# Window attention and two feed-forward layers on one core: both groups' products together in a visit, and three engines tied to the program's order

## The chip, the cores and the metric

The kernel runs on one core of one Trainium2 chip. The metric is the device time of one execution in microseconds (us). The core's engines are TensorE (PE: matmuls and transposes, with its weight loads as PEld), VectorE (DVE), ScalarE (ACT), GpSimd (POOL) and SyncE (SP, which here issues every DMA). Each takes its instructions from a queue of its own, and semaphores make one engine wait for another.

## The reference

Three layers follow each other. Attention with 4 batches, 8 heads, 576 positions and 64 channels, in which each position sees itself and the 63 before it; then x (2304 x 512) goes through a layer with three input matrices and an elementwise maximum, and through a second layer with a quadratic gate.

```python
scores = scale * np.matmul(q, k.transpose(0, 1, 3, 2))
mask = (rel >= 0) & (rel < window)                 # window = 64
attn = softmax(np.where(mask, scores, -1e9))
x = np.matmul(attn, v)                             # as 2304 tokens x 512
h = np.maximum(np.maximum(x @ w1, x @ w2), x @ w3) # 2304 x 768
x2 = h @ w_out                                     # 2304 x 512
h2 = x2 @ w_in                                     # 2304 x 2048
g = np.where(h2 >= 1, h2, np.where(h2 <= -1, 0, (h2 + 1) ** 2 / 4))
out = g @ w_out2
```

## The kernel before

Matmuls are in float32; each operand of a dense layer is split into a rounded high part and a rest, and three of the four products are taken. The first layer works on nine blocks of 256 tokens. For a block, 18 `a_item`s (line 357; 12 matmuls each, into one of three PSUM tiles `ps` of the pool `pmm`) make three products per slice f of the hidden layer. The first is copied out by ACT (`ht`), the other two are taken into a maximum by DVE (line 372), and a sixth of h is then split by ACT and POOL. Four `b_item`s (line 380; 18 matmuls) make x2, which ACT copies to one of two buffers `x2s` and SP stores to memory. The second layer (lines 536 to 633) works on blocks of 512 tokens; its weights are split by ACT, DVE and POOL (`w_split`, line 154), as those of the first layer are in the first 90 us.

Attention works on 36 groups of 64 positions (all heads). A group passes through load, `prep` (transposes of q and k, by PE for the first 16 groups, by DVE from `raw` tiles for the others), `qk` (line 275: 16 small matmuls for four pairs of heads into `sps2`; then DVE reads each pair, adds the mask and keeps the row's extreme in `nm`), `ex` (ACT, four exponentials), `norm` (DVE, then POOL multiplies), `ptr` and `ptc` (PE transposes, ACT copies to `pt`), and `pv` (line 334: 16 small matmuls into `ops2`; ACT copies the high part to the block's `xt`, DVE writes the rest). `sps2` takes two PSUM banks: a group's four pairs are spread over both, and the two groups of a visit stand in the same banks. `ops2` is one bank for both groups.

Groups 8 to 35 go through in 14 pairs. A list `order` holds pieces of work with a position each (an `a_item` takes 1, a `b_item` 1.5), and pairs are put at `visits` (line 505), 6 apart at first and then 12. At one visit stand PV of one pair, the transposes of the next, and QK of the one after. The list is sorted, and from the first visit on `chained` (line 549) keeps PE's instructions in the list's order (`issue_after`: order in the queue only, no wait). The other engines' orders are left to a scheduler that simulates the time. The tile framework lets two engines use one PSUM bank only after each other: it adds a semaphore wait wherever one follows the other in the list.

Of the kernel before, what the change touches and what calls it, by code (L numbers as in the profile page):

```python
# [9 lines left out]
F32 = mybir.dt.float32  # L10
# [24 lines left out]
BD = 6  # L35
# [10 lines left out]
VISITS = (-24, -18, -12)  # L46
VSTEP = 12
VLEAD = 2
EXP = (1.1, 2.1)
PTC = (0.6, 1.6)  # L50


# [8 lines left out]
def kernel(ctx, tc, q, k, v, w1, w2, w3, wo1, wi2, wo2, out, x2d):  # L61
# [12 lines left out]
    nc = tc.nc  # L74
# [7 lines left out]
    P = 128  # L82
    BL = 64
    NBB = S // BL
    NG = B * NBB
    NP = H // 2
# [20 lines left out]
    def act_copy(dst, src, scale=1.0):  # L107
        nc.scalar.activation(dst, src, AF.Copy, scale=scale)  # L108

    def sub(eng, dst, a, b):  # L110
        eng.tensor_tensor(dst, a, b, op=ALU.subtract)  # L111

    def f32(ap):
        return ap.bitcast(F32)
# [12 lines left out]
    apool = att_stack.enter_context(tc.tile_pool(name="apool", bufs=1, side="right", reuse_waits="tile"))  # L127
# [8 lines left out]
    ops2 = patt.tile([P, 2, NP, BL], F32, name="ops2")  # L136
# [37 lines left out]
    def w_col(key, hl, kt):  # L174
        return wslot[key][:, hl * 512 + kt * P: hl * 512 + (kt + 1) * P]


    st_g = defaultdict(dict)
# [4 lines left out]
    def blk(g):  # L183
        b, i = divmod(g, NBB)
        return b, i, g % 4

    def natural(g):
        return g % 4 != 0
# [77 lines left out]
    def window(g):  # L266

        b, i, s = blk(g)
        if i == 0:
            return lambda r, p: kring[r, p, s, :], maskA[:, BL:2 * BL], BL  # L270
        if natural(g):
            return lambda r, p: kring[r, p, s - 1:s + 1, :], maskA, 2 * BL
        return lambda r, p: kring[r, p, 0::3, :], maskB, 2 * BL

    def qk(g):
        d = st_g[g]
        win, mask, W = window(g)
        sm = apool.tile([P, NP, 2 * BL], F32, tag="sm", name="sm", bufs=5)
        nm = apool.tile([P, NP], F32, tag="nm", name="nm", bufs=5)


        for x in range(2):
            for bank in range(2):
                p = 2 * bank + x
                for h in range(2):
                    r = slice(h * BL, h * BL + BL)
                    o = (h ^ bank) * BL
                    nc.tensor.matmul(  # L288
                        sps2[o:o + BL, bank, g % 2, x, 0:W], d["q"][r, p, :], win(r, p), start=True, stop=True
                    )  # L290

        for p in range(NP):
            nc.vector.tensor_tensor_reduce(  # L293
                out=sm[:, p, 0:W], in0=sps2[:, p // 2, g % 2, p % 2, 0:W], in1=mask, scale=-QSCALE, scalar=BIG,
                op0=ALU.add, op1=ALU.min, accum_out=nm[:, p:p + 1],
            )
        d.update(sm=sm, nm=nm, W=W)

    def ex(g):
        d = st_g[g]  # L300
        W, sm = d["W"], d["sm"]
        ss = apool.tile([P, NP], F32, tag="ss", name="ss", bufs=5)
        for p in range(NP):
            nc.scalar.activation(  # L304
                sm[:, p, 0:W], sm[:, p, 0:W], AF.Exp, bias=d["nm"][:, p:p + 1], scale=-1.0, accum_out=ss[:, p:p + 1]
            )
        d["ss"] = ss

    def norm(g):
        d = st_g[g]  # L310
# [20 lines left out]
        act_copy(pt[0:W], d["pps"][0:W])  # L331
        d["pt"] = pt

    def pv(g, xt, off):
        d = st_g[g]
        W, pt, vr = d["W"], d["pt"], st_g[max(g, 1)]["vr"]
        ops = ops2[:, g % 2]
        for p in range(NP):
            for h in range(2):
                r = slice(h * BL, h * BL + BL)  # L340
                o = (h ^ p // 2) * BL
                nc.tensor.matmul(  # L342
                    ops[r, p, :], vr[0:W, 2 * p + h, :], pt[0:W, p, o:o + BL], start=True, stop=True
                )
        act_copy(xt[:, 0, :, off:off + BL], ops)
        sub(nc.vector, xt[:, 1, :, off:off + BL], ops, f32(xt[:, 0, :, off:off + BL]))


    xts = {}
    hts = {}  # L350

    def xt_new(j):
        xts[j] = fpool.tile([P, 2, NP, N1], F32R, tag="xt", name="xt", bufs=3)
# [41 lines left out]
    def x2_split(tb, pool, kt):  # L395
        t0, n = blocks2[tb]
        if kt == 0:
            x2t[tb] = pool.tile([P, 2, KD, N2], F32R, tag="x2t", name="x2t", bufs=1)
        x = x2t[tb]
        r = pool.tile([P, N2], F32, tag="x2r", name="x2r", bufs=2)  # L400
        nc.sync.dma_start(r[:, 0:n], x2d[kt, :, t0:t0 + n])
        act_copy(x[:, 0, kt, 0:n], r[:, 0:n])
        sub(nc.vector, x[:, 1, kt, 0:n], r[:, 0:n], f32(x[:, 0, kt, 0:n]))
# [23 lines left out]
        for o in range(0, n, BL):  # L427
            gblock[(t0 + o) // BL] = (j, o)

    def pv_x(g):  # L430
        j, o = gblock[g]
        if o == 0:
            xt_new(j)
        pv(g, xts[j], o)


    order = []
# [1 line left out]
    def put(at, fn, *args):  # L439
        order.append((at, len(order), fn, args))  # L440
# [13 lines left out]
    def a_items(j):  # L454
        return [(1.0, a_item, (j, f, w)) for f in range(KF1) for w in range(3)]

    def b_items(j):
        return [(1.5, b_item, (j, dt)) for dt in range(KD)]

    seq, first = [], a_items(1)  # L460
# [4 lines left out]
    late = b_items(0)  # L465
    for j in range(1, len(blocks1)):
        items = first if j == 1 else a_items(j)
        seq += items[:BD] + late + items[BD:]
        late = b_items(j)
    seq += late  # L470
    at, begin = 0.0, {}
# [9 lines left out]
    def ptr_c(g):  # L481
        ptr(g)
        ptc(g)

    stages = (load, vload, prep, qk, ex, norm, ptr_c, pv_x)
    ops0 = dict(L=load, V=vload, P=prep, Q=qk, E=ex, N=norm, T=ptr_c, X=pv_x)
    for x, tok in enumerate(SEQ.split()):
        if tok[0] == "W":
            for _ in range(int(tok[1:] or 1)):
# [3 lines left out]
    for j in range(1, PB):  # L493
# [4 lines left out]
        for m in range(n1):  # L498
            g = t1 // BL + m
            at = lo + (m + 1) * (hi - lo) / n1  # L500
            for x, fn in enumerate(stages):
                y = LP if x == 0 and g in pet else STAGES[x]
                put(at + y, fn, g)
    g0 = blocks1[PB][0] // BL
    visits = [begin[PB] + x for x in VISITS]
    while len(visits) < (NG - g0) // 2 + 2:
        visits.append(begin[PB] - VLEAD + VSTEP * (len(visits) - len(VISITS)))
    for x, g1 in enumerate(range(g0, NG, 2)):
        vq, vt, vp = (visits[x + y] + 0.2 for y in range(3))
        for y in range(2):  # L510
            g = g1 + y
            put(vq + (LP if g in pet else STAGES[0]), load, g)
            put(vt, vload, g)
            put(vq + STAGES[2], prep, g)
            put(vq + 0.02, qk, g)
            put(vq + EXP[y], ex, g)
            put(vq + EXP[y] + 1, norm, g)
            put(vt + 0.01, ptr, g)
            put(vt + PTC[y], ptc, g)
            put(vp, pv_x, g)  # L520
    put(begin[len(blocks1) - 1] - 0.1, None)

    order2 = [(w, f) for f in range(KF2) for w in (4, 5)]
# [2 lines left out]
    def w2_next():  # L526
        n = w2n[0]
        if n < len(order2):
            w, f = order2[n]
            st = w_load((w, f), wi2 if w == 4 else wo2, slots2[n], "col" if w == 4 else "row", f)  # L530
            w_split((w, f), st, nc.gpsimd)
            w2n[0] += 1
# [3 lines left out]
    def c_mm(tb, f, pool=pmm, tag="mm"):  # L536
        n = blocks2[tb][1]
        ps = hps[tb, f] = pool.tile([P, 512], F32, tag=tag, name="hp")
        passes = [(kt, wl, xl) for kt in range(KD) for wl, xl in ((0, 0), (0, 1), (1, 0))]
        for x, (kt, wl, xl) in enumerate(passes):  # L540
            nc.tensor.matmul(  # L541
                ps[:, 0:n], w_col((4, f), wl, kt), x2t[tb][:, xl, kt, 0:n],
                start=(x == 0), stop=(x == len(passes) - 1),
            )

    order.sort(key=lambda e: e[:2])
    tail = [None]

    def chained(fn, *args):

        if tail[0] is None:
            fn(*args)
        else:
            with tc.issue_after(tail[0]):
                fn(*args)
        pe = [i for i in nc.cur_bb.bb.instructions[-200:] if i.engine == mybir.EngineType.PE]
        if pe:
            tail[0] = pe[-1]

    for at, _, fn, args in order:  # L560
        if fn:
            if (fn, args) == (b_item, (len(blocks1) - 1, 0)):
                c_mm(0, 0, pacc, "acc")
            if at < visits[0]:
                fn(*args)
            else:
                chained(fn, *args)
        else:
            att_stack.close()
            p2 = ctx.enter_context(tc.tile_pool(name="p2", bufs=1, side="right", reuse_waits="tile"))  # L570
            pacc = ctx.enter_context(tc.tile_pool(name="pacc", bufs=5, space=PSUM))
            slots2 += [p2.tile([P, 1024], F32R, name=f"v{i}") for i in range(2 * KF2 - NU)] + U
            for kt in range(KD):
                x2_split(0, p2, kt)
            for _ in range(4):
                w2_next()
# [41 lines left out]
    seq = [(tb, f) for tb in range(len(blocks2)) for f in range(KF2)]  # L618
# [40 lines left out]
```

## Time and profile before

| | |
|---|---|
| median of 3 runs | 863.98 us (861.62 to 864.16) |
| the profiled execution | 864.39 us |
| its span, first to last instruction | 862.3 us |
| PE busy | 798.3 us (93%) |
| DVE, ACT, POOL busy | 363.9, 356.2, 157.9 us |
| mean granted clock of TensorE | 0.985 |

The span is the time from the first to the last instruction of the profiled execution; some 2 us of its time lie around it. Busy time is an engine's sum over its instructions. An idle time is told with its releaser, the instruction of another engine whose end let the waiting one start. The kernel has three stretches: until about 100 us weights are split beside the first blocks; from 100 to 400 us the first layer runs with two visits per block; after it the second layer, until 480 us beside the splits of its weights.

### The profile page before, as it was taken

Reading aid. Unit: us, or ns where it says so; the run is one execution under the profiler, and the core shown is the slowest. Engines: PE = TensorE matmul, PEld = TensorE weight load, DVE = VectorE, ACT = ScalarE, POOL = GpSimd, SP = SyncE. Lnnn points to the kernel's source line nnn. Section 1 sums busy time; section 2 is a strip of 40 time slices with the busy share of each in tenths; the row PEclk is TensorE's granted clock in tenths of the full one; section 3 lists DMA queues with packets and bytes.
Section 4 is the critical chain, followed back from the end, with each engine's and each line's share of the span. In section 5 each row is a group of like instructions: output and inputs, shape, how many; then the busy total and the mean of one; then the engine's idle time right before and its main releaser. Section 6 shows DMA issues by size and latency. Waiting matters only on the chain.

```text
span 862.3 us, 14835 instructions
## 1 busy us (share of the span) xinstructions
PE 798.3 (93%) x5776; PEld 701.6 (81%) x5776; DVE 363.9 (42%) x937; ACT 356.2 (41%) x871; POOL 157.9 (18%) x157
## 2 busy tenths in 40 slices
PE   6698889999999898999779999999999999999998
PEld 4597778889898888898778888888888888888896
DVE  5778422323333432316678733433343334333343
ACT  6988533333333534324779422322232223222232
POOL 3666311111111121213574200000000000000000
PEclk8899999999999999999989999999999999999999
DMA  9976243233141413003777000100020001000000
GB/s 243 279 216 187 43 84 85 52 70 63 40 80 32 135 26 98 14 26 111 234 222 241 24 1 25 62 0 1 1 74 0 1 1 36 25 1 1 24 26 25
DMA packets 128054, 62.70 MB, mean 73 GB/s; under 512 B 98288, under 2 KB 120816, under 8 KB 127984
## 3 DMA queue, kind: packets, MB, share of 16 engines
q1 hardware_dynamic: 127984, 61.76, 26.2%
q8 instruction: 45, 0.74, 0.4%
q14 instruction: 25, 0.20, 0.1%
HBM read 52.30 MB, written 9.44 MB: 72 GB/s over the span
## 4 chain that ended last, share of the span: by engine, by line
PE 77%; DVE 5%; DMA 4%; ACT 4%; issue 2%; SPq 1%; POOL 1%; DVEq 0%; ACTq 0%; POOLq 0%
PE acc L606 23%; PE hp L541 23%; PE ps L363 18%; PE ps L385 7%; DMA wst<-in_moe_w_in 3%; PE ops L342 2%; PE sps L288 2%; PE pps L324 1%; DVE sm L293 1%; SPq L215 1%; DVE wt L170 1%; DMA x2r<-x_scratch 1%; ACT wst L165 1%; DVE wt L169 1%; ACT wst L108 1%
## 5 line engine op out<-in xcount | busy, mean ns | idle before, releaser
L363 PE MATMUL ps<-xt,u 128*128 128x256 f32 x1944 | 239.1, 283 | 9.1 <-DVE ht L372 4.0
L363 PEld LDWEIGHTS ps<-xt,u 128*128 128x128 f32 x1944 | 232.5, 190 | 13.9 <-DVE ht L372 5.2
L541 PE MATMUL hp<-x2t,u 128*128 128x512 f32 (+1 forms) x720 | 161.6, 372 | 0.0
L606 PE MATMUL acc<-u,g 128*128 128x512 f32 x648 | 160.4, 396 | 0.0
L586 ACT ACTIVATE u<-hp,half 128x512 f32<-128x512 f32 (+1 forms) x80 | 51.5, 644 | 251.6 <-PE hp L541 251.5
L541 PEld LDWEIGHTS hp<-x2t,u 128*128 128x128 f32 x720 | 126.9, 188 | 27.2
L606 PEld LDWEIGHTS acc<-u,g 128*128 128x128 f32 x648 | 120.9, 188 | 28.3
L589 DVE SCALAR_TENSOR_TENSOR gt<-u,hp 128x512 f32<-128x512 f32 (+1 forms) x80 | 50.6, 632 | 165.8 <-ACT u L587 165.7
L372 DVE TENSOR_TENSOR ht<-ps,ht 128x256 f32<-128x256 f32 x108 | 45.4, 421 | 131.3 <-PE ps L363 114.0
L385 PE MATMUL ps<-h,u 128*128 128x256 f32 x648 | 82.8, 287 | 4.8 <-ACT h L108 2.4
L385 PEld LDWEIGHTS ps<-h,u 128*128 128x128 f32 x648 | 79.7, 194 | 7.2 <-ACT h L108 2.6
L111 POOL TENSOR_TENSOR u<-wt,u 128x512 fp32r<-128x512 f32 x48 | 67.5, 1408 | 46.7 <-ACT u L108 44.3
L111 POOL TENSOR_TENSOR h<-ht,h 128x256 fp32r<-128x256 f32 x54 | 42.7, 793 | 129.0 <-ACT h L108 128.7
L315 POOL TENSOR_TENSOR sm<-sm,rs 128x512 f32<-128x512 f32 (+1 forms) x36 | 35.8, 994 | 142.4 <-DVE rs L314 130.3
L304 ACT ACTIVATE sm<-sm,nm 128x128 f32<-128x128 f32 (+1 forms) x144 | 55.2, 388 | 15.2 <-DVE nm L293 15.2
L170 DVE CUSTOM_DVE_ANT_0 wt<-wst,wt 128x1024 uint16<-128x1024 uint16 x56 | 56.2, 1004 | 3.5 <-ACT wst L108 0.6
L108 ACT ACTIVATE h<-ht 128x256 fp32r<-128x256 f32 x54 | 22.3, 414 | 83.7 <-DVE ht L372 83.6
L606 PE MATMUL acc<-v,g 128*128 128x512 f32 x216 | 53.6, 394 | 0.0
L541 PE MATMUL hp<-x2t,v 128*128 128x512 f32 (+1 forms) x240 | 53.5, 371 | 0.0
L593 DVE CAST g<-gt 128x512 fp32r<-128x512 f32 (+1 forms) x80 | 34.2, 428 | 45.5 <-PE acc L606 43.1
L111 DVE TENSOR_TENSOR g<-gt,g 128x512 fp32r<-128x512 f32 (+1 forms) x80 | 51.1, 639 | 2.7
L541 PEld LDWEIGHTS hp<-x2t,v 128*128 128x128 f32 x240 | 41.9, 188 | 8.3
(50 smaller groups left out, 627.6 us busy)
## 6 DMA issues: line engine op xcount, KB each, us to landing
wst<-in_moe_w_out SPq DMA_DIRECT2D x22, 512.0 KB, 4.4
wst<-in_moe_w SPq DMA_DIRECT2D x18, 512.0 KB, 5.7
wst<-in_moe_w_in SPq DMA_DIRECT2D x16, 512.0 KB, 4.3
vr<-in_v SPq DMA_DIRECT2D x24, 256.0 KB, 3.0
x_scratch<-x2s SPq DMA_DIRECT2D x36, 128.0 KB, 1.8
out<-ob SPq DMA_DIRECT2D x18, 256.0 KB, 2.0
x2r<-x_scratch SPq DMA_DIRECT2D x16, 256.0 KB, 2.9
vr<-in_v SPq DMA_DIRECT2D x19, 128.0 KB, 3.4
```

The costliest lines, as they stand in the source:

```text
L111: eng.tensor_tensor(dst, a, b, op=ALU.subtract)
L170: nc.vector.tensor_tensor(t, t, lo, op=ALU.add)
L304: nc.scalar.activation(sm[:, p, 0:W], sm[:, p, 0:W], AF.Exp, bias=d["nm"][:, p:p + 1], scale=-1.0, accum_out=ss[:, p:p + 1])
L315: nc.gpsimd.tensor_tensor(sm[:, :, 0:W], sm[:, :, 0:W], rs.unsqueeze(2).to_broadcast([P, NP, W]), op=ALU.mult)
L363: nc.tensor.matmul(ps[:, 0:n], w_col((w, f), wl, kt), xt[:, xl, kt, 0:n], start=(x == 0), stop=(x == len(passes) - 1))
L372: nc.vector.tensor_tensor(t[:, 0:n], ps[:, 0:n], part[j, f][:, 0:n], op=ALU.max)
L385: nc.tensor.matmul(ps[:, 0:n], w_col((3, f), wl, dt), hts[j, f][:, xl, 0:n], start=(x == 0), stop=(x == len(passes) - 1))
L541: nc.tensor.matmul(ps[:, 0:n], w_col((4, f), wl, kt), x2t[tb][:, xl, kt, 0:n], start=(x == 0), stop=(x == len(passes) - 1),)
L586: nc.scalar.activation(u[:, 0:n], ps[:, 0:n], AF.Relu, bias=half, scale=2.0 ** (-WS / 2 - 1))
L589: nc.vector.scalar_tensor_tensor(gt[:, 0:n], u[:, 0:n], 2.0 ** WS, ps[:, 0:n], op0=ALU.min, op1=ALU.max)
L593: nc.vector.tensor_copy(g[:, 0, 0:n], gt[:, 0:n])
L606: nc.tensor.matmul(accs[t], g[:, gl, t * P:(t + 1) * P], wslot[5, f][:, wl * 512:(wl + 1) * 512], start=(f == 0 and x == 0), stop=(f == KF ...
```

## The change

`qk` and `pv` lose their reads. The reads of QK become `red`, called for two pairs of heads at a time and placed 0.3 and 1.3 (first group) and 2.3 and 3.3 (second) after the visit; the exponentials also go two pairs at a time, at 1.7, 2.7, 3.7 and 4.7 (before: all four at 1.1 and all four at 2.1); `norm` comes at 3.7 and 5.7 (before 2.1 and 3.1). The reads of PV become `values`, one ACT copy and one DVE subtraction for both groups. `chained` now ties ACT and DVE to the list's order as well as PE, for all work from the first visit on; what stood before it goes in ahead. Since order on ACT then counts, the x2 items of block 0 move four `a_item`s earlier (`bd = 2`). The first product of the second layer, `c_mm(0, 0)`, is tied too: its 12 matmuls stand together ahead of the last block's x2 items, where the scheduler had spread them among earlier ones.

```diff
-EXP = (1.1, 2.1)
+RED = (0.3, 2.3)
+EXP = (1.7, 3.7)
...
-        for p in range(NP):
+    def red(g, pairs=range(NP)):
+        ...
+        for p in pairs:
             nc.vector.tensor_tensor_reduce(
                 out=sm[:, p, 0:W], in0=sps2[:, p // 2, g % 2, p % 2, 0:W], in1=mask, scale=-QSCALE, scalar=BIG,
...
-    def pv(g, xt, off):
+    def pv(g):
...
-        act_copy(xt[:, 0, :, off:off + BL], ops)
-        sub(nc.vector, xt[:, 1, :, off:off + BL], ops, f32(xt[:, 0, :, off:off + BL]))
+    def values(g, n, xt, off):
+
+        o = ops2[:, g % 2:g % 2 + n].rearrange("a g p c -> a p g c")
+        hl = [xt[:, x, :, off:off + n * BL].rearrange("a p (g c) -> a p g c", g=n) for x in range(2)]
+        act_copy(hl[0], o)
+        sub(nc.vector, hl[1], o, f32(hl[0]))
...
-        seq += items[:BD] + late + items[BD:]
+        bd = 2 if j == 1 else BD
+        seq += items[:bd] + late + items[bd:]
...
-            put(vq + EXP[y], ex, g)
-            put(vq + EXP[y] + 1, norm, g)
+            for z in range(2):
+                put(vq + RED[y] + z, red, g, (2 * z, 2 * z + 1))
+                put(vq + EXP[y] + z, ex, g, (2 * z, 2 * z + 1))
+            put(vq + EXP[y] + 2, norm, g)
...
-            put(vp, pv_x, g)
+            put(vp, pv, g)
+        put(vp + 0.04, val, g1, 2)
...
-    def chained(fn, *args):
-
-        if tail[0] is None:
+    tails = defaultdict(list)
+
+    def chained(fn, *args, tie=True):
+
+        ends = {}
+        with ExitStack() as stack:
+            for i in [i for e in tails for i in tails[e]] if tie else ():
+                stack.enter_context(tc.issue_after(i))
+            n = len(nc.cur_bb.bb.instructions)
             fn(*args)
...
+        for i in nc.cur_bb.bb.instructions[n:]:
+            if i.engine in TIED:
+                ends[i.engine] = i
+        for e, i in ends.items():
+            tails[e] = [i] if tie else tails[e] + [i]
+
+    TIED = (mybir.EngineType.PE, mybir.EngineType.Activation, mybir.EngineType.DVE)
...
-                c_mm(0, 0, pacc, "acc")
-            if at < visits[0]:
-                fn(*args)
-            else:
-                chained(fn, *args)
+                chained(c_mm, 0, 0, pacc, "acc")
+            chained(fn, *args, tie=at >= visits[0])
```

On PE a visit's rows are the same before and after (16 matmuls into `ops`, 8 transposes into `pps`, 16 matmuls into `sps`); what changes is which reads the program puts between them. ACT's queue at the visit with x2 items, before and then after (`xt` is the high part of PV, `pt` the transposed probabilities, `sm` the exponentials, `x2s` the x2 copies, `ht` and `h` the first layer's):

```order
L108 ACTIVATE x2s<-ps 128x256 x3
L108 ACTIVATE xt<-ops_103 128x4x64 x2
L108 ACTIVATE pt<-pps 128x512 x2
L304 ACTIVATE sm,ss<-sm,nm 128x128 x8
L108 ACTIVATE x2s<-ps 128x256
L108 ACTIVATE ht_2095<-ps 128x256
```

```order
L109 ACTIVATE x2s<-ps 128x256 x3
L109 ACTIVATE xt<-ops_103 128x4x128
L109 ACTIVATE x2s<-ps 128x256
L109 ACTIVATE pt<-pps 128x512 x2
L312 ACTIVATE sm,ss<-sm,nm 128x128 x2
L109 ACTIVATE ht_2083<-ps 128x256
L312 ACTIVATE sm,ss<-sm,nm 128x128 x4
L109 ACTIVATE h<-ht_2160 128x256
```

Two copies of PV became one of twice the width; the fourth x2 copy moved ahead of the `pt` copies, and the eight exponentials are now broken up by copies of the first layer.

SP's queue where block 0's x2 is stored and the first `raw` tiles (groups 16 to 19) are loaded, before and then after:

```order
L215 DMA raw<-in_q 32x4x32 x25
L215 DMA raw<-in_k 32x4x32 x11
L390 DMA x_scratch<-x2s 128x256
L215 DMA raw<-in_k 32x4x32 x21
L390 DMA x_scratch<-x2s 128x256
```

```order
L216 DMA raw<-in_q 32x4x32 x21
L216 DMA raw<-in_k 32x4x32 x16
L402 DMA x_scratch<-x2s 128x256
L216 DMA raw<-in_k 32x4x32 x5
L402 DMA x_scratch<-x2s 128x256
```

The first x2 store stands behind 48 of the 64 small loads instead of 43, the second behind five more instead of 21, while the x2 items themselves moved four `a_item`s forward on PE.

DVE's queue after, near the end of the first visit (groups 8 and 9; `ss`, `rs` is `norm`, `wt` a weight split; the second `ss`, `rs` is that of group 9):

```order
L320 TENSOR_SCALAR ss<-ss 128x4
L321 RECIPROCAL rs<-ss 128x4
L384 TENSOR_TENSOR ht_1172<-ps,ht_1104 128x256
L170 TENSOR_SCALAR wt<-wst 128x512
L171 ISA wt<-wst,wt 128x1024
L384 TENSOR_TENSOR ht_1201<-ps,ht_1132 128x256
L320 TENSOR_SCALAR ss<-ss 128x4
L321 RECIPROCAL rs<-ss 128x4
```

Between the two groups' `norm` stand two maxima of the first layer and one weight split; before, the two stood with one maximum among them and ahead of the last two splits.

## Rows read from the trace of the kernel before

**Rows 1.** Busy time of the engines, from the page.

```profile
PE 798.3 (93%) x5776; PEld 701.6 (81%) x5776; DVE 363.9 (42%) x937; ACT 356.2 (41%) x871; POOL 157.9 (18%) x157
```

**Rows 2.** Stretches: length, busy us (instructions) by engine, clock, DMA share, GB/s.

```profile
140.00:160.00 20.00, 18.00 (x196) 17.08 (x195) 6.01 (x30) 7.76 (x27) 3.14 (x4) 1.00 0.31 69
...
480.00:500.00 20.00, 20.00 (x88) 16.14 (x87) 11.38 (x19) 5.76 (x10) 3.62 (x3) 1.00 0.00 1
```

**Rows 3.** PE's waits from 118 to 398 us: total, times, longest.

```profile
PE ops L342 <- DVE xt L111: 12.2, 13, 0.9
PE sps L288 <- DVE nm L293: 11.3, 11, 1.1
PE ps L363 <- ACT ht L108: 1.2, 1, 1.2
PE ps L363 <- ACT x2s L108: 0.3, 1, 0.3
```

**Rows 4.** One visit in order of time: start, length, engine, line, operation [idle before].

```profile
144.77 0.69 PE L342 MATMUL ops<-pt,vr 128*64 128x64 f32 x16
...
145.50 0.38 ACT L108 ACTIVATE xt<-ops 128x256 fp32r<-128x256 f32 x1 [0.19 <-PE ops L342]
...
145.92 0.42 DVE L111 TENSOR_TENSOR xt<-ops,xt 128x256 fp32r<-128x256 f32 x1 [6.86 <-ACT xt L108]
...
146.40 0.69 PE L342 MATMUL ops<-pt,vr 128*64 128x64 f32 x16 [0.94 <-DVE xt L111]
...
149.76 0.67 PE L288 MATMUL sps<-kring,qt 64*64 64x128 f32 x16 [1.06 <-DVE nm L293]
```

**Rows 5.** PE's waits from 60 to 118 us.

```profile
PE sps L288 <- DVE nm L293: 4.3, 3, 2.2
PE tp L249 <- ACT x2s L108: 2.2, 1, 2.2
...
PE ops L342 <- DVE xt L111: 0.9, 1, 0.9
```

**Rows 6.** PE in order of time, just after block 0's x2.

```profile
112.52 2.96 PE L363 MATMUL ps<-xt,u 128*128 128x256 f32 x24
```

**Rows 7.** SP, ACT and DVE in order of time, x2 stores among loads.

```profile
98.42 5.12 SPq L215 DMA_DIRECT2D raw<-in_k  x11
...
103.63 1.58 SPq L390 DMA_DIRECT2D x_scratch<-x2s  x1
...
115.30 0.38 SPq L390 DMA_DIRECT2D x_scratch<-x2s  x1
...
117.22 0.38 ACT L108 ACTIVATE x2s<-ps 128x256 f32<-128x256 f32 x1 [5.48 <-DMA x_scratch<-x2s]
...
117.97 0.42 DVE L372 TENSOR_TENSOR ht<-ps,ht 128x256 f32<-128x256 f32 x1 [8.11 <-ACT ht L108]
```

**Rows 8.** Groups by line, whole span: busy, mean ns | idle before, releaser.

```profile
L315 POOL TENSOR_TENSOR sm<-sm,rs 128x512 f32<-128x512 f32 (+1 forms) x36 | 35.8, 994 | 142.4 <-DVE rs L314 130.3
L304 ACT ACTIVATE sm<-sm,nm 128x128 f32<-128x128 f32 (+1 forms) x144 | 55.2, 388 | 15.2 <-DVE nm L293 15.2
L170 DVE CUSTOM_DVE_ANT_0 wt<-wst,wt 128x1024 uint16<-128x1024 uint16 x56 | 56.2, 1004 | 3.5 <-ACT wst L108 0.6
L108 ACT ACTIVATE h<-ht 128x256 fp32r<-128x256 f32 x54 | 22.3, 414 | 83.7 <-DVE ht L372 83.6
...
L108 ACT ACTIVATE wst<-wst 128x512 int32<-128x512 uint32 x56 | 37.5, 669 | 0.0
```

**Rows 9.** PE in order of time at the last two blocks' x2 items.

```profile
408.09 2.37 PE L385 MATMUL ps<-h,u 128*128 128x256 f32 x18 [0.64 <-ACT ht L108]
...
448.18 0.80 PE L385 MATMUL ps<-h,u 128*128 128x256 f32 x2 [2.37 <-ACT h L108]
449.37 9.16 PE L385 MATMUL ps<-h,u 128*128 128x256 f32 x55 [0.39 <-POOL h L111]
```

**Rows 10.** The stretch just after, columns as in rows 2.

```profile
450.00:455.00 5.00, 5.00 (x26) 5.00 (x26) 2.24 (x4) 3.89 (x9) 2.11 (x3) 0.52 0.89 286
```

More of the change, by code (lines that the diff above doesn't have):

```diff
@@ L290, in qk @@
                     )
-        for p in range(NP):
+        d.update(sm=sm, nm=nm, W=W)
+    def red(g, pairs=range(NP)):
+        d = st_g[g]
+        _, mask, W = window(g)
+        sm, nm = d["sm"], d["nm"]
+        for p in pairs:
             nc.vector.tensor_tensor_reduce(
@@ L296, in qk, with ex @@
             )
-        d.update(sm=sm, nm=nm, W=W)
-    def ex(g):
+    def ex(g, pairs=range(NP)):
         d = st_g[g]
         W, sm = d["W"], d["sm"]
-        ss = apool.tile([P, NP], F32, tag="ss", name="ss", bufs=5)
-        for p in range(NP):
+        if pairs[0] == 0:
+            d["ss"] = apool.tile([P, NP], F32, tag="ss", name="ss", bufs=5)
+        ss = d["ss"]
+        for p in pairs:
             nc.scalar.activation(
@@ L306, in ex @@
             )
-        d["ss"] = ss
     def norm(g):
@@ L428, with val @@
             gblock[(t0 + o) // BL] = (j, o)
-    def pv_x(g):
+    def val(g, n=1):
         j, o = gblock[g]
@@ L433, in pv_x, with qk_r @@
             xt_new(j)
-        pv(g, xts[j], o)
+        values(g, n, xts[j], o)
+    def pv_x(g):
+        pv(g)
+        val(g)
+    def qk_r(g):
+        qk(g)
+        red(g)
     order = []
@@ L483, in ptr_c @@
         ptc(g)
-    stages = (load, vload, prep, qk, ex, norm, ptr_c, pv_x)
-    ops0 = dict(L=load, V=vload, P=prep, Q=qk, E=ex, N=norm, T=ptr_c, X=pv_x)
+    stages = (load, vload, prep, qk_r, ex, norm, ptr_c, pv_x)
+    ops0 = dict(L=load, V=vload, P=prep, Q=qk_r, E=ex, N=norm, T=ptr_c, X=pv_x)
     for x, tok in enumerate(SEQ.split()):
@@ L546 @@
     order.sort(key=lambda e: e[:2])
-    tail = [None]
-    def chained(fn, *args):
-        if tail[0] is None:
-            fn(*args)
-        else:
-            with tc.issue_after(tail[0]):
-                fn(*args)
-        pe = [i for i in nc.cur_bb.bb.instructions[-200:] if i.engine == mybir.EngineType.PE]
-        if pe:
-            tail[0] = pe[-1]
+    tails = defaultdict(list)
[5 more added lines that the diff above has]
+            n = len(nc.cur_bb.bb.instructions)
+            fn(*args)
+        for i in nc.cur_bb.bb.instructions[n:]:
[4 more added lines that the diff above has]
+    TIED = (mybir.EngineType.PE, mybir.EngineType.Activation, mybir.EngineType.DVE)
     for at, _, fn, args in order:
@@ L562 @@
             if (fn, args) == (b_item, (len(blocks1) - 1, 0)):
-                c_mm(0, 0, pacc, "acc")
-            if at < visits[0]:
-                fn(*args)
-            else:
-                chained(fn, *args)
+                chained(c_mm, 0, 0, pacc, "acc")
+            chained(fn, *args, tie=at >= visits[0])
         else:
```

## Prediction

> **What bounds the kernel now.** I read the page's busy times first: PE is busy for 93% of the span and no other engine for more than 42% [rows 1]. So a change counts where it touches PE's waits. The stretches show where they lie. In the second layer PE is busy for 20.00 of 20 us; in the first layer beside attention for 18.00 of 20, at full clock, with DVE at 6.01 and ACT at 7.76 [rows 2]. The list of waits then names the missing 2 us. From 118 to 398 us PE waits 13 times before the second group's PV products for DVE's write to `xt`, 12.2 us, and 11 times before the second group's QK products for DVE's read of `sps`, 11.3 us; all else there is two waits of 1.2 and 0.3 us [rows 3]. The order of time of one visit shows the mechanism: the first PV products, then ACT's copy, DVE's subtraction, and only then, after 0.94 us idle, the second PV products; QK likewise with 1.06 us [rows 4]. The two groups use different columns, but the same banks, and the program reads the first group's results between the two.
>
> **The change part by part.** The times below are against the profiled execution (864.4 us: span 862.3 and some 2 around it), which is 0.4 above the median.
>
> *Products together, reads after, 118 to 398 us.* Nothing is read between the two groups' products any more, so both waits go: 12.2 + 11.3 = 23.5 us. The bank is next written at the following visit, 12 units later, so no new wait of that kind is near. What could be late next? The first item of a block needs `xt`. The merged copy and subtraction are twice as wide as the rows' 0.38 and 0.42 us [rows 4]; at twice the time they end some 1.8 us after the products, and behind those stand 24 more transposes and QK products and one item before `xt` is used, over 3 us of PE work. The softmax chain now ends 2.6 units later than before, since the exponentials stand between copies of the first layer on ACT. Its last `norm` is at 5.7 of 12 units; about half of the time to the next visit, some 20 us (12 items of 1.48 [rows 6] and the visit's own products), is left for DVE, POOL's 0.99 us [rows 8] and slips. The fourth x2 copy stands ahead of the `pt` copies on ACT, which then wait some 3 us for its matmuls; they are needed a visit later. ACT and DVE have 12 us free in 20. So I cost ties and later chains at nothing there. If that cover were gone at every visit, the bounds are nothing and the whole 23.5 us.
>
> *The first visits, 60 to 118 us.* Here waits of the same kinds are 4.3 and 0.9 us, and PE also waits 2.2 us for an x2 copy [rows 5]: 7.4 us that could go. But two new delays arise. First, the visits are 6 units apart here, and the second group's `norm` at 5.7 stands right before its transposes at 6.0. Ahead of that `norm` in the tied queues stands one weight split. From the end of the item before: a maximum 0.42 [rows 7], the h copy 0.41, two ACT passes on the weights 2 x 0.67, DVE's sum 1.00, ACT's copy of it (as 0.67), two exponentials 0.78, `norm` (tiny; as 0.35), POOL 0.99 [rows 8] make about 6.0 us. PE has two items (2.96 for 24 matmuls [rows 6]) and a first set of transposes (some 0.5) in that time, so it waits about 2.5 us. Second, x2. Block 0's items move four items earlier, but their stores do not: the first stands behind 48 small loads, five more than before, at 0.47 us each (5.12 for 11 [rows 7]). Before, the first store was issued at 103.63 and the second, 21 loads later, at 115.30; the third ACT copy waited 5.48 us for a buffer and PE 2.18 [rows 5, 7]. After, the first store goes at about 106.0 and the second at 108.9, and with the 1.9 us from the second's issue to the copy that it frees [rows 7] the fourth x2 copy can start at about 110.8. Behind it on ACT stand two `pt` copies, four exponentials, two first-layer copies: about 3.7 us. Three `ps` tiles hold that much back; the item that started at 112.52 [rows 6] then starts at about 114.6, but the 2.18 us wait behind it is gone. If the loads begin sooner, as the earlier split that frees their buffer suggests, the store moves up with them, by up to 2.5 us. So what was gained before this point is absorbed by SP's loads: a gain of 0 to 2.5 us, of which I take 1. The ends for the range are a gain of 7.4 (all of rows 5's three waits) and a loss of 4 (the 2.5 of the transposes in full, and 1.5 for a late copy).
>
> That last step rests on ACT holding everything behind a waiting copy. Rows 7 show it: while ACT waited 5.48 us, DVE's maximum waited 8.11 us for the `ht` copy behind it. [...] Where ACT could let the `pt` and `ht` copies pass, the term would be 7.4 - 2.5 = 4.9 us of gain and the sum 836.0; by the rule it is 1 and the sum 839.9. [...]
>
> *c_mm(0, 0) moved, 396 to 466 us.* Its 12 matmuls leave places in which they filled PE's time and come to stand just ahead of the last x2 items, where PE waited 2.37 and 0.39 us for h [rows 9]. At 0.23 us each (88 in 20.00 us [rows 2]) they are 2.8 us, which is about what that wait would hide. In their old places PE then reaches the next waits sooner and waits there longer, at most by the same 2.8. I take nothing; the ends are a gain of 5.4 and a loss of 2.8. [...]
>
> The sum: 864.4 - 23.5 - 1.0 + 0 = 839.9 for the profiled execution, and 839.5 beside the median.
>
> **The rivals.**
>
> *A: the deeper gain.* The wait before the last x2 items goes together with the dip of the clock (5.4), or the early waits go in full (6.4 more than taken). For it: both are in the rows. Against it: weight splits hold ACT and DVE in both stretches. Time: 864 - 23.5 - 1 - 5.4 = 834, and 828 with both.
>
> *B: the tie gives part back.* ACT and DVE in the list's order meet a wait at every block: a weight or x2 buffer that comes later than the list assumes, with evictions behind it, and the three `ps` tiles run out. The nearest price is the 2.18 us of rows 5; at each of the seven blocks with attention that is 15 us. A share of it, 6 to 12 us, gives 846 to 852. For it: loads of `raw` start later, since their buffers are freed by transposes that are now tied to three units before a visit. Against it: the transposes need them 20 us and more later, and other engines are idle for 12 us in 20.
>
> *C: slower than before.* The store of x2 falls behind the small loads in every block with loads, as in rows 7: ACT stands still for 5 us, then `xt` is late as well and PE waits for both. It decides from the point at which the new waits pass 24.5 us: five chunks of loads at 5.48 us are 27.4, so 864 - 24.5 + 27.4 = 867. For it: 64 loads at 0.47 us are 30 us of SP in a block of two visits, some 40. Against it: in the later chunks stores were not late before, and the program puts stores among the loads at about the time at which x2 is ready.
>
> *D: the change does not do what it says.* If the second products still waited for some read of the same bank, as of the previous pair, the time would be 864 - 0 to 2. Against it: that read ends some 10 us earlier.
>
> **How the numbers follow.** My forecast, 839.5 us, has 0.60, with a range of its own from 835 to 845 (the ends of the early stretch). A has 0.15, B 0.17, C 0.04, D 0.04. The range from 830 to 852 holds the forecast, most of A and most of B. About 0.3%, 2.6 us, is what a measurement of this kernel can tell from no change. Faster takes the forecast, A and B and some of D: 0.94. Same takes most of D: 0.03. Slower takes C, less what of it stays within 2.6 us: 0.03.
>
> **What would show it.** Right: in the list of PE's waits the pairs `ops` for `xt` and `sps` for `nm` are gone, or have fewer than 4 us left, and stretches between 120 and 370 us show PE at 19.5 of 20 or more; the second layer's 20 us stretches are as before, only earlier. Early on I expect a wait of `pps` for POOL of 2 to 3 us, and one of `ps` for ACT near 110 us. Wrong: waits of `ps` for ACT or DVE at each visit (B), ACT's x2 copies waiting for stores in several blocks (C), the old two waits under another releaser (D). If PE is as full as I say and the time falls by less than 15 us, the sum of the second layer's stretches has grown, which nothing here foresees.

## The result, and the profile after

The changed kernel takes 838.03 us (median of 4 runs, 836.24 to 838.96), beside 862.80 for the kernel before on the same chip: a ratio of 0.971, 95% interval 0.968 to 0.974. The forecast was 839.5. The total agrees; of its terms, as the parts below show, one was too small and one had the wrong sign.

The page's busy times after, to be read beside [rows 1]; the span is 837.2 us, so PE is at 95% instead of 93% with no less work in the list:

```profile
PE 793.8 (95%) x5776; PEld 701.5 (84%) x5776; DVE 363.1 (43%) x923; ACT 348.8 (42%) x857; POOL 157.5 (19%) x157
```

PE's waits from 118 to 390 us (total, times, longest), which answer to [rows 3]. Both named waits are gone:

```profile
PE ps L375 <- ACT ht L109: 2.6, 1, 2.6
PE ps L397 <- DVE ht L384: 0.8, 2, 0.5
```

The stretch 140 to 160 us, in the columns of [rows 2]: PE is busy for all of it, with 218 matmuls where there were 196. The stretch 480 to 500 us is as before.

```profile
140.00:160.00 20.00, 20.00 (x218) 19.46 (x217) 6.11 (x30) 7.55 (x27) 3.44 (x5) 1.00 0.19 51
...
480.00:500.00 20.00, 20.00 (x87) 16.10 (x86) 6.12 (x10) 5.28 (x8) 0.00 (x0) 1.00 0.00 0
```

One visit of PE in order of time (start, length, engine, line, operation), to be read beside [rows 4]. Both groups' products are one row of 32, and no row has an idle time behind it (the trace has two entries for each small matmul of the program, so the 16 that the part ahead counts for a visit are 32 here):

```profile
147.18 1.15 PE L349 MATMUL ops<-pt,vr 128*64 128x64 f32 x32
148.26 1.09 PE L331 MATMUL pps<-ident,sm 128*128 128x128 f32 x8
149.28 1.10 PE L289 MATMUL sps<-kring,qt 64*64 64x128 f32 x32
150.32 1.90 PE L397 MATMUL ps<-h,u 128*128 128x256 f32 x14
```

The first visits went the other way. PE's waits from 60 to 118 us, beside [rows 5], are other waits and longer in sum (10.6 us, beside 9.3 with the one of 1.9 us that [rows 5] leave out):

```profile
PE ps L375 <- DVE ht L384: 4.1, 2, 2.2
PE pps L331 <- POOL sm L322: 2.8, 1, 2.8
PE ps L375 <- ACT ht L109: 2.2, 1, 2.2
PE tp L250 <- ACT ht L109: 1.5, 1, 1.5
```

To add this up, the span is cut at two starts that every kernel of this study has: PE's first matmul on `ops` in the second visit with PV of the 14 pairs (122.89 us before, 127.74 after), and in the last such visit (393.04 and 371.05). The three stretches, from profiled executions, in us:

| kernel | early: to 2nd PV | steady: 2nd to last PV | late: to the end | span | median time |
|---|---|---|---|---|---|
| before | 122.9 | 270.2 | 469.3 | 862.3 | 862.8 |
| changed | 127.7 | 243.3 | 466.2 | 837.2 | 838.0 |
| difference | +4.8 | -26.8 | -3.1 | -25.1 | -24.8 |
| forecast | -1.0 | -23.5 | 0 | -24.5 | -24.5 |

The late stretch shows what the prediction said of `c_mm` and the clock. PE around the last x2 items (idle before, releaser in brackets), beside [rows 9] (the first row is for a comparison further down): the waits are 1.74 and 0.31 us instead of 2.37 and 0.39, and the 55 matmuls behind them take 6.68 us instead of 9.16.

```profile
405.23 4.47 PE L375 MATMUL ps<-xt,u 128*128 128x256 f32 x36 [0.90 <-ACT ht L109]
...
416.15 2.90 PE L565 MATMUL hp<-x2t,v 128*128 128x512 f32 x12
...
422.54 0.50 PE L397 MATMUL ps<-h,u 128*128 128x256 f32 x2 [1.74 <-ACT h L109]
423.35 6.68 PE L397 MATMUL ps<-h,u 128*128 128x256 f32 x55 [0.31 <-POOL h L112]
...
439.45 3.03 PE L631 MATMUL acc<-v,g 128*128 128x512 f32 x12 [1.24 <-DVE g L618]
444.14 3.06 PE L565 MATMUL hp<-x2t,u 128*128 128x512 f32 x12 [1.66 <-DVE gt L614]
```

The granted clock is 1.00 from 425 to 430 us, where [rows 10] had 0.52. But two new waits stand behind it, 1.24 and 1.66 us in the second layer, for DVE.

### The profile page after: what moved, and what is told of

Same layout as the page of the kernel before. It is cut to its first block, busy times and chain, and to the rows that moved or that the text cites. A ratio compares the mean times of both kernels' runs of the same rounds, so it can differ in the third digit from the quotient of the medians.

```text
span 837.2 us, 14780 instructions
## 1 busy us (share of the span) xinstructions
PE 793.8 (95%) x5776; PEld 701.5 (84%) x5776; DVE 363.1 (43%) x923; ACT 348.8 (42%) x857; POOL 157.5 (19%) x157
## 3 DMA queue, kind: packets, MB, share of 16 engines
q1 hardware_dynamic: 127984, 61.76, 26.8%
## 4 chain that ended last, share of the span: by engine, by line
PE 78%; DVE 4%; issue 3%; POOL 2%; ACT 2%; DMA 2%; SPq 0%; DVEq 0%; POOLq 0%; ACTq 0%
PE acc L631 24%; PE hp L565 23%; PE ps L375 20%; PE ps L397 7%; POOL u L112 2%; PE ops L349 2%; DMA wst<-in_moe_w_in 2%; PE pps L331 2%; PE sps L289 2%; DVE wt L170 1%; DVE wt L171 1%; DMA x2r<-x_scratch 1%; ACT wst L166 1%; ACT u L109 1%; DVE x2t L112 1%
## 5 line engine op out<-in xcount | busy, mean ns | idle before, releaser
L397 PE MATMUL ps<-h,u 128*128 128x256 f32 x648 | 80.4, 281 | 2.8 <-ACT h L109 1.7
L397 PEld LDWEIGHTS ps<-h,u 128*128 128x128 f32 x648 | 77.2, 188 | 4.7 <-ACT h L109 1.9
L170 DVE TENSOR_SCALAR wt<-wst 128x512 int32<-128x512 int32 x56 | 38.9, 695 | 25.0 <-POOL u L112 14.4
```

The lines of the kernel that those rows point to most:

```text
L170: nc.vector.tensor_scalar(t, hi, 3, None, op0=ALU.logical_shift_left)
L397: nc.tensor.matmul(ps[:, 0:n], w_col((3, f), wl, dt), hts[j, f][:, xl, 0:n], start=(x == 0), stop=(x == len(passes) - 1))
```

## The experiments

All start from the changed kernel, and each was timed beside the kernel before on one chip (862.0 to 863.0 us there). The last section of this part puts them in one table.

### Is it the ties or the place of x2 that costs the early stretch?

The first theory: the ties of ACT and DVE, through the weight splits in their queues. The second: x2 held by its stores, as the prediction had it. The first experiment ties PE alone.

```diff
-    TIED = (mybir.EngineType.PE, mybir.EngineType.Activation, mybir.EngineType.DVE)
+    TIED = (mybir.EngineType.PE,)
```

> The changed kernel, but with PE alone tied to the list's order; ACT and DVE are left to the scheduler as in the kernel before. Theory 1 (the gain is the products standing together; the tie is only an order): the steady stretch from the visit of groups 14 and 15 to the last one keeps its 243 us, and the early stretch, where tied queues hold evictions behind weight splits, gives back up to 5 us: 833 to 838 us. Rival (the tie is what makes the gain, by keeping ACT and DVE from blocking evictions with bursts of eight exponentials): waits of ps for ACT at every visit, 850 us or more.

Measured: 830.20 us, ratio to before 0.963 (0.961 to 0.965). It beats both kernels, and all that it gains on the changed one is early: the second PV starts at 117.7 instead of 127.7 us, the steady stretch takes 243.8 instead of 243.3. PE in 60 to 100 us shows where, first in the changed kernel and then with PE tied alone (stretch, then busy us of PE, PEld, DVE, ACT, POOL, clock):

```profile
60.00:80.00 20.00, 17.06 (x152) 16.14 (x150) 16.94 (x24) 14.17 (x28) 12.56 (x10) 0.91 0.81 237
80.00:100.00 20.00, 12.36 (x101) 11.17 (x102) 9.45 (x36) 12.43 (x37) 8.16 (x8) 0.86 0.31 58
```

```profile
60.00:80.00 20.00, 17.65 (x170) 16.68 (x168) 19.29 (x39) 17.02 (x43) 12.88 (x11) 1.00 0.80 240
80.00:100.00 20.00, 17.93 (x191) 16.80 (x192) 14.64 (x40) 14.05 (x44) 11.44 (x10) 1.00 0.35 74
```

With three ties, DVE and ACT do less in 60 to 80 us, and from 80 to 100 us PE runs 101 matmuls instead of 191, at a clock of 0.86 instead of 1.00. From the first visit with PV (108.67 and 98.62 us) to the second, both kernels take the same 19.07 us, so the 10.0 us lie before it: 0.9 ahead of the first tied products (QK at 75.14 and 74.26), 6.2 in waits (four with 8.6 us in sum, shown further down, against two with 2.4), and 3.0 in matmuls that ran at a lower clock behind such waits.

Next the ties of ACT and DVE begin only at position 36, after the splits (PE is tied as before), and the x2 items go back to their old place:

```diff
-        bd = 2 if j == 1 else BD
-        seq += items[:bd] + late + items[bd:]
+        seq += items[:BD] + late + items[BD:]
...
-            chained(fn, *args, tie=at >= visits[0])
+            chained(fn, *args, tie=TIED if at >= 36 else TIED[:1] if at >= visits[0] else ())
```

> The changed kernel, but ACT and DVE are tied only from position 36 of the list on (PE from the first visit as before), and block 0's x2 items stand where they stood in the kernel before. Theory 1 (the tied queues cost the early stretch, in which PE arrives 4.9 us later at the visit of groups 14 and 15 than before): the early stretch is that of before less its product waits; 830 to 834 us. Rival (the early stretch is late for another reason, as the later norm of the first visits or the SP queue's loads): 837 to 840.

Measured: 835.63 us (0.968 to 0.972 of before), slower than was expected. The longest of PE's waits from 60 to 118 us shows the reason:

```profile
PE tp L250 <- ACT x2s L109: 4.5, 1, 4.5
...
```

The first visit with PV starts at 99.3 us, as with PE tied alone, but the second at 124.3: there an x2 copy was waited for 4.5 us. So I expected the old place of the x2 items to cost these 4.5 us with PE tied alone as well, and tried it:

```diff
-    TIED = (mybir.EngineType.PE, mybir.EngineType.Activation, mybir.EngineType.DVE)
+    TIED = (mybir.EngineType.PE,)
...
-        bd = 2 if j == 1 else BD
-        seq += items[:bd] + late + items[bd:]
+        seq += items[:BD] + late + items[BD:]
```

> The PE-tied kernel e1, with block 0's x2 items back at their place of the kernel before (six items of block 1 ahead of them instead of two). Theory 2 (in that place the third x2 copy waits for a store behind SP's small loads, and PE for it, 4.5 us in e4): the wait of the transposes for ACT's x2 copy is back near 112 us, 834 to 836 us against e1's 830.2. Rival (the 4.5 us of e4 came from the tie's late begin): 830 us, no such wait.

Measured: 830.35 us, the same as with the new place. The second theory fell as a cause by itself: with PE tied alone the x2 wait of PE is 1.7 us in 60 to 118 us, and it costs nothing that the medians show. But the last two runs differ only in the ties of ACT and DVE from position 36 on, and these cost 5.3 us. From the first visit with PV (99.3 us) to 109 us both run alike to 0.1 us, and in both SP issues the second x2 store late, at 114.1 and 114.4 us. Then ACT's order parts them, first with the ties from 36, then with PE tied alone:

```profile
116.02 0.38 ACT L109 ACTIVATE x2s<-ps 128x256 f32<-128x256 f32 x1 [7.78 <-DMA x_scratch<-x2s]
116.30 0.38 ACT L109 ACTIVATE ht<-ps 128x256 f32<-128x256 f32 x1
```

```profile
110.70 0.39 ACT L109 ACTIVATE ht<-ps 128x256 f32<-128x256 f32 x1 [2.44 <-PE ps L375]
...
117.53 0.38 ACT L109 ACTIVATE x2s<-ps 128x256 f32<-128x256 f32 x1 [4.46 <-DMA x_scratch<-x2s]
```

Tied, the `ht` copy stands behind an x2 copy that waits 7.78 us for that store; left to the scheduler, it goes ahead. So the late store costs where the tie puts what PE needs behind it. No weight split of the first layer is involved there: the last one's sum on DVE starts at 88.39 us.

Which tie is it? Two runs leave one of them out:

```diff
-    TIED = (mybir.EngineType.PE, mybir.EngineType.Activation, mybir.EngineType.DVE)
+    TIED = (mybir.EngineType.PE, mybir.EngineType.Activation)
```

> PE and ACT are tied, DVE is left to the scheduler; all else as in the changed kernel. Theory 1a (the 10 us that the three ties cost before 118 us come from ACT's queue: the tied `u` copies of the weight splits wait there for DVE's sums, 8.1 us in the changed kernel against 2.8 with PE tied alone, and the `ht` copies stand behind them): about 836, and the waits of `ps` for DVE and ACT between 60 and 118 us stay. Rival 1b (they come from DVE's queue, where maxima and `ss` wait behind splits): 830 to 832. Rival 1c (it takes both ties): 831 to 834.

```diff
-    TIED = (mybir.EngineType.PE, mybir.EngineType.Activation, mybir.EngineType.DVE)
+    TIED = (mybir.EngineType.PE, mybir.EngineType.DVE)
```

> PE and DVE are tied, ACT is left to the scheduler. Theory 1a (ACT's tie costs the 10 us): 830 to 832. Rival 1b (DVE's tie does): about 836. Rival 1c (it takes both): 831 to 834. The steady stretch, from the second visit's PV to the last, stays at 243 to 244 us under each of them.

Measured: 839.08 us with ACT tied (ratio 0.971 to 0.976), 833.82 with DVE tied (0.965 to 0.970). ACT's tie alone costs all of it, 8.9 us against 830.20, as theory 1a has it, though 3 us more than it says; DVE's alone costs 3.6, for which 1a has no place and which is too little for 1b; together they cost 7.8, so the two prices don't add. The waits of ACT from 60 to 118 us, with ACT tied, with DVE tied, and with neither:

```profile
ACT u L109 <- DVE wt L171: 9.4, 8, 2.8
ACT x2s L109 <- DMA x_scratch<-x2s: 5.6, 2, 4.3
```

```profile
ACT sm L312 <- DVE nm L300: 5.0, 4, 2.2
ACT u L109 <- DVE wt L171: 4.3, 5, 1.9
```

```profile
ACT u L109 <- DVE wt L171: 2.8, 5, 0.9
```

One such wait in the changed kernel, ACT in order of time:

```profile
80.25 0.63 ACT L109 ACTIVATE u<-wt 128x512 fp32r<-128x512 f32 x1 [2.77 <-DVE wt L171]
80.79 0.37 ACT L109 ACTIVATE ht<-ps 128x256 f32<-128x256 f32 x1
```

A tied weight copy waits 2.77 us for DVE's sum, the `ht` copy that frees a `ps` tile stands behind it, and PE then waits 2.18 us for that copy (the row at 81.21 below).

The `ht` copies are not the whole of it. With ACT tied, PE's longest wait before 118 us is 5.32 us, for the second group's probabilities: their exponentials, too, stand behind a weight copy that waits for DVE. ACT, then PE:

```profile
92.49 0.63 ACT L109 ACTIVATE u<-wt 128x512 fp32r<-128x512 f32 x1 [2.22 <-DVE wt L171]
...
95.77 1.06 PE L331 MATMUL pps<-ident,sm 128*64 128x128 f32 x4 [5.32 <-POOL sm L322]
```

How the 8.9 us divide between these chains is not shown by a run.

### What are the products together worth, part by part?

The PV part undone (each group's copy and subtraction between the products again):

```diff
-            put(vp, pv, g)
-        put(vp + 0.04, val, g1, 2)
+            put(vp, pv_x, g)
```

> The changed kernel with the PV part undone: each group's PV products are followed by its own ACT copy and DVE subtraction again. Theory 1 prices a PV pair by start to start times, 2.25 us before and 1.08 after: 14 pairs give 16.4 us back, 854 us; the list of PE's waits has 14 of 0.94 for xt again. Rival (a pair is worth its listed wait alone, 0.94): 13.2 us, 851.

The QK part undone:

```diff
-            put(vq + 0.02, qk, g)
+            put(vq + 0.02, qk_r, g)
             for z in range(2):
-                put(vq + RED[y] + z, red, g, (2 * z, 2 * z + 1))
```

> The changed kernel with the QK part undone: each group's reads by DVE follow its own QK products; exponentials stay two pairs at a time. Theory 1 prices a QK pair by start to start times, 2.32 us before and 1.04 after: 11 to 14 pairs give 14 to 18 us back, 852 to 856 us. Rival (listed wait alone, 1.05): 11.5 to 14.7, 849.5 to 852.5.

Measured: 858.02 and 858.62 us, 20.0 and 20.6 more than the changed kernel (ratio to before 0.996 for both); more than expected for both. PE's waits from 118 to 385 us, PV part undone and then QK part undone:

```profile
PE ops L349 <- DVE xt L112: 15.0, 12, 2.9
```

```profile
PE sps L289 <- DVE nm L300: 13.2, 11, 2.9
```

The old waits came back with the old counts, but the longest is 2.9 us, where [rows 3] had 0.9 and 1.1: under the ties the read between the products can itself be late. Then both undone, ties kept, and both undone with PE tied alone (both edits above; for the second, also the first experiment's):

> The changed kernel with both the PV and the QK part undone: reads follow each group's products again, but ACT and DVE are tied and the exponentials go two pairs at a time. Theory 1 with the prices of e2 and e3 (20.0 and 20.6 us against the changed kernel): 838.0 + 40.6 = 878.6, 872 to 880 us, so the tie by itself is a loss of 10 us or more against the kernel before. Rival (the two undone parts share their cost, since either leaves one wait per visit that hides the other's): 858 to 866 us.

> PE alone is tied, and each group's reads stand between the products again (both parts undone), with the chain of exponentials, bd = 2 and the tied first product of the second layer as in the changed kernel. It prices the products together where the ties are no longer in it. If a pair of products costs its start-to-start difference (1.17 and 1.28 us by 26 pairs in all 32 us): 830.2 + 32 = 862, about the kernel before. If the ties cost what the full-tie run without both parts showed (886.5) and not only the 10 us early, this stands far under it: the difference of the two is then the ties' price with the reads between, some 24 us. If it is 855 or less, the products together are worth less than the steady stretch says.

Measured: 886.51 us (ratio 1.025 to 1.030, slower than before) and 862.73 us (0.998 to 1.001, the same as before). So the products together are worth 862.73 - 830.20 = 32.5 us with PE tied alone, as expected from the pairs, and 48.5 with all three tied; I had expected 872 to 880 for the tied one and missed it. What it adds is seen early. PE, then ACT, of that kernel in order of time:

```profile
108.67 0.69 PE L349 MATMUL ops<-pt,vr 128*64 128x64 f32 x16
115.32 1.12 PE L349 MATMUL ops<-pt,vr 64*64 64x64 f32 x16 [5.97 <-DVE xt L112]
```

```profile
114.15 0.38 ACT L109 ACTIVATE x2s<-ps 128x256 f32<-128x256 f32 x1 [5.55 <-DMA x_scratch<-x2s]
114.43 0.38 ACT L109 ACTIVATE xt<-ops 128x256 fp32r<-128x256 f32 x1
```

ACT waits 5.55 us for an x2 store, the `xt` copy stands behind it, and PE, which needs that read before its next products, waits 5.97 us. This is the mechanism of the prediction's rival C, and with the ties and the reads between the products it is real. With the products together PE doesn't need the read there. The early stretch is 15.0 us longer than with PE tied alone (table below), the steady one 8.1.

Last of this part, whether it matters that reads and exponentials go in pieces: PE tied alone, all four pairs of a group at once, with the exponentials and `norm` at the places of the kernel before.

```diff
-EXP = (1.7, 3.7)
+EXP = (1.1, 2.1)
...
-            for z in range(2):
-                put(vq + RED[y] + z, red, g, (2 * z, 2 * z + 1))
-                put(vq + EXP[y] + z, ex, g, (2 * z, 2 * z + 1))
-            put(vq + EXP[y] + 2, norm, g)
+            put(vq + 0.03, red, g)
+            put(vq + EXP[y], ex, g)
+            put(vq + EXP[y] + 1, norm, g)
```

> The PE-tied kernel e1, with the reads of a group's scores in one piece right after the products and the exponentials of a group in one piece at the places of the kernel before (1.1 and 2.1, norm one later); what is left of the change is that the products of both groups stand together, one value copy for both, and block 0's x2 items. Theory 1 (that alone is the gain): 829 to 832 us. Rival (bursts of eight exponentials hold evictions, so the pieces matter): waits of ps for ACT at the visits, 834 us or more.

Measured: 830.12 us. The pieces are worth nothing here; the order of PE's products is the gain.

### Is the late gain the first product of the second layer?

```diff
-                chained(c_mm, 0, 0, pacc, "acc")
+                c_mm(0, 0, pacc, "acc")
```

> The changed kernel with the second layer's first product left to the scheduler, which spreads its 12 matmuls over earlier gaps. Theory 3 (its place ahead of the last x2 items hides the wait for h there and avoids the clock's fall behind it; the stretch to the second layer is 5 us shorter and 2 to 3.4 us come back behind it): 840 to 842 us, a wait of about 2.4 us for h again and a low clock behind it. Rival (that stretch is shorter for another reason, and the place is worth nothing): 838 us.

Measured: 836.59 us, not slower than the changed kernel (ratios to before 0.968 to 0.974 for both). Left to the scheduler, the wait before the last x2 items is back at 2.06 us, and the 55 matmuls take 8.18 us instead of 6.68. But the waits of 1.24 and 1.66 us in the second layer are gone, and the late stretch is 466.3 us against 466.2. The theory that this place is worth the late gain fell: what it gains is given back within some 20 us.

### All runs side by side

| kernel | early | steady | late | span | median |
|---|---|---|---|---|---|
| changed | 127.7 | 243.3 | 466.2 | 837.2 | 838.03 |
| PE tied alone | 117.7 | 243.8 | 465.8 | 827.3 | 830.20 |
| the same, old place of x2 | 119.6 | 242.1 | 466.6 | 828.3 | 830.35 |
| the same, whole groups | 117.8 | 245.4 | 465.1 | 828.3 | 830.12 |
| ACT, DVE tied from 36, old place of x2 | 124.3 | 244.0 | 466.7 | 835.0 | 835.63 |
| PE and ACT tied | 127.5 | 240.4 | 467.9 | 835.8 | 839.08 |
| PE and DVE tied | 123.5 | 242.8 | 468.8 | 835.1 | 833.82 |
| PV part undone | 127.4 | 261.3 | 466.9 | 855.7 | 858.02 |
| QK part undone | 131.0 | 258.9 | 466.0 | 856.0 | 858.62 |
| both undone, three ties | 138.8 | 277.7 | 469.4 | 885.9 | 886.51 |
| both undone, PE tied alone | 123.8 | 269.6 | 467.2 | 860.6 | 862.73 |
| first product left free | 125.3 | 242.7 | 466.3 | 834.3 | 836.59 |

Stretches are from one execution each and their spans lie 0.6 to 3.3 us below the medians, but for the run with DVE tied (1.3 above): differences under 3 us are not read from one of them.

## Why the prediction was right, and where it was wrong

**What bounds, and the mechanism: right.** Undoing either part brought its wait back with its count (12 and 11). Rival D fell. The cover for `xt` held, though the 24 transposes and QK products that I counted behind PV are 40 entries in the trace (8 and 32): they take 2.1 us (148.26 to 150.32), with one item of the first layer still over 3 us.

**Steady stretch: right mechanism, the term too small** (-23.5 forecast, -26.8 measured). I counted the idle time that the list of waits shows. A pair costs more than that, by the distance of starts, from a pair's first matmul to the next operation on PE. Of the visit in [rows 4], these are the rows of PE between and behind those shown there:

```profile
147.02 1.09 PE L324 MATMUL pps<-ident,sm 128*128 128x128 f32 x8
148.04 0.67 PE L288 MATMUL sps<-kring,qt 64*64 64x128 f32 x16
...
150.36 0.86 PE L385 MATMUL ps<-h,u 128*128 128x256 f32 x5
```

A PV pair took 2.25 us before (144.77 to 147.02) and takes 1.08 after (147.18 to 148.26, in the visit shown above): 1.17 less, where the list names 0.94. A QK pair took 2.32 (148.04 to 150.36) and takes 1.04: 1.28 less for a listed 1.06. The 12 PV and 11 QK pairs between the marks make 14.0 + 14.1 = 28.1 us; less the new `ht` wait of 2.6 us, where waits of 1.2 and 0.3 were before, that is 27.0. So each interruption cost some 0.22 us beyond its idle time. Over 23 pairs that is 0.22 x 23 = 5.1 us more than the listed idle. The rows show it too: two rows of 16 matmuls took 0.69 us each before, the row of 32 took 1.15 after. What makes this part is not shown by a run.

**First visits: the step failed** (1 us of gain forecast, 4.8 of loss measured; 1.0 of it lies ahead of the first tied products, at 75.14 instead of 74.09 us, so the loss is about the end of 4 that I gave). What I named, I sized well, but for a wait of `ps` for ACT near 110 us, which did not come: `pps` waited 2.8 us for POOL (2.5 forecast), and SP issued the first two x2 stores at 106.07 and 108.93 us (106.0 and 108.9 forecast). But the stores did not hold PE up in the changed kernel. SP in order of time, and ACT's third x2 copy, which was to wait:

```profile
106.07 0.38 SPq L402 DMA_DIRECT2D x_scratch<-x2s  x1
...
108.93 0.38 SPq L402 DMA_DIRECT2D x_scratch<-x2s  x1
```

```profile
108.83 0.38 ACT L109 ACTIVATE x2s<-ps 128x256 f32<-128x256 f32 x1 [0.23 <-ACT sm L312]
```

It waited 0.23 us, since PE itself came late. What failed is "what was gained before this point is absorbed by SP's loads": what sets the stretch lies up to 25 us earlier, where I had costed one weight split ahead of one `norm` and no other eviction behind a split. PE there, in the changed kernel:

```profile
81.21 1.67 PE L375 MATMUL ps<-xt,u 128*128 128x256 f32 x12 [2.18 <-ACT ht L109]
84.36 1.09 PE L250 MATMUL tp<-ident,nat 128*128 128x128 f32 x8 [1.48 <-ACT ht L109]
87.65 5.90 PE L375 MATMUL ps<-xt,u 128*128 128x256 f32 x36 [2.20 <-DVE ht L384]
...
96.74 0.63 PE L331 MATMUL pps<-ident,sm 128*64 128x128 f32 x4 [2.75 <-POOL sm L322]
```

Three waits for `ht` that the prediction does not have, and then 36 matmuls in 5.90 us that take 4.47 us elsewhere (at 405.23). Tying PE alone removes 10.0 us of the early stretch (7.8 of the median), and the two runs with one tie put the larger part on ACT's queue. So the early waits of [rows 5] could indeed be gained (6.1 us between both undone and PE tied alone, 123.8 to 117.7), and the tie took more than that. That is rival B's mechanism. It also came once in the steady stretch, where the second layer's weights are split: it is the new `ht` wait of 2.6 us. ACT, then PE:

```profile
297.39 0.66 ACT L166 ACTIVATE wst<-wst 128x512 f32<-128x512 f32 x1 [3.86 <-DMA wst<-in_moe_w_in]
...
300.46 4.47 PE L375 MATMUL ps<-xt,u 128*128 128x256 f32 x36 [2.60 <-ACT ht L109]
```

A weight pass waits 3.86 us for its load, and the `ht` copy of 300.04 us stands behind it. With PE and DVE tied such a wait is 2.0 us, with PE alone or PE and ACT there is none above 0.2 us.

**c_mm and the late stretch** (0 forecast, -3.1 measured). That its place is worth nothing was right. No run shows as a gain the 2.6 us by which the end of 5.4 exceeds the 2.8 of the 12 matmuls, and which rival A has for the dip of the clock: the 55 matmuls took 6.68 us instead of 9.16, with the clock at 1.00 from 425 to 430 us, but 1.24 and 1.66 us of new waits stand behind them. Of the 3.1 us, 1.2 is the last visit's PV pair, which I had counted to the steady term. The rest stays open: the late stretch lies between 465.1 and 469.4 us in all kernels, and no run here ties 2 us of it to one edit.

**The sum** came out because the errors cancel: 5.8 us too good early, 6.4 too little in the other two. The forecast's own range held; the reasons for its middle did not.

## What to carry to other kernels

Where two products share a bank and a read of the first stands between them, issue both and then read: here that was 32.5 us, and a pair was worth the distance of starts (1.17 and 1.28 us), not the listed idle time (0.94 and 1.06). Tie an engine's queue to the program only where nothing in it waits for work that the tie does not order for the bottleneck; PE tied alone kept all of the gain, and ACT tied as well gave 8.9 us of it back. A weight split was such work here (a copy waited 2.77 us for its sum), and so was a store behind small loads (7.78 us). If ties have to stay, what PE needs at once should not hang on a read in such a queue: with the reads between, the same ties made the kernel slower than before.

## What the runs showed of the hardware

In the visit of [rows 4], an interruption of PE between two groups of 16 small matmuls cost 0.22 to 0.23 us beyond its idle time (1.28 us for a listed 1.06, 1.17 for 0.94; 23 of them lie in the steady stretch). And the granted clock fell behind a stretch in which PE stood still much of the time. The two stretches, in the changed kernel:

```profile
84.00:88.00 4.00, 1.44 (x9) 1.21 (x10) 2.70 (x11) 3.18 (x12) 1.57 (x2) 0.92 0.43 90
88.00:92.00 4.00, 4.00 (x25) 4.00 (x25) 1.63 (x8) 2.47 (x11) 2.47 (x3) 0.65 0.50 97
```

PE is busy for 1.44 of 4 us, and in the next 4 the clock is 0.65 while PE is fully busy: 25 matmuls ran, where the 36 of the same kind at 405.23 us, in 4.47, make 32. In the kernel before, a visit with a wait of 0.94 and one of 1.06 us left the clock at 1.00 from 140 to 160 us [rows 2, 4], and every other 20 us from 120 to 400 have 1.00 as well.

The list of waits alone does not tell whether the clock falls. Ahead of the first tied products PE makes eight transposes and then waits 1.91 or 1.92 us for the same maximum of DVE in all 13 kernels of this study. The 36 matmuls behind that wait took 6.0 us in the profiled execution of seven of them and 4.5 in that of six. The kernel before, at a clock of 0.64 from 68 to 72 us, and the one with PE tied alone, at 1.00 from 60 to 80:

```profile
68.13 6.03 PE L363 MATMUL ps<-xt,u 128*128 128x256 f32 x36 [1.91 <-DVE ht L372]
```

```profile
69.86 4.48 PE L375 MATMUL ps<-xt,u 128*128 128x256 f32 x36 [1.92 <-DVE ht L384]
```

What decides between the two stays open; it puts up to 1.6 us into a stretch of one execution that no edit made.
